# Half-height matmuls in pairs: a routed two-expert layer whose first product runs part of its terms on two halves of the TensorE array

## The chip, the cores and the metric

The kernel runs on one core of a Trainium2 chip. The metric is the device time of one execution in microseconds (us), the median of several runs.

## What is computed

The reference is a causal convolution over a sequence, followed by a mixture of experts in which each token goes to two of eight experts:

```python
# x: (8, 3584, 192), weight: (8 heads, 7 taps)
w = softmax(weight)                        # over the taps
x = causal_conv(x, w)                      # (28672 tokens, 192)
noisy = x @ w_gate + log1p(exp(x @ w_noise)) * noise    # (28672, 8)
top2, top2_w = two largest of noisy, softmax over the two
for e in range(8):
    for k in range(2):
        mask = top2[:, k] == e
        h = np.maximum(x[mask] @ w1[e], 0.0)            # 192 -> 1024
        out[mask] += top2_w[mask, k, None] * (h @ w2[e])  # 1024 -> 192
```

All inputs and outputs are float32.

## The kernel before

**The stages.** The 28672 tokens are split into 28 units of 1024. A unit is convolved (mostly on VectorE, DVE), scaled, split into float16 high and low parts in a tile `rb`, gated (eight small matmul groups on TensorE, PE, at line 485, and some 50 small DVE instructions), and its rows are scattered by indirect DMAs of GpSimd (POOL) into a DRAM buffer `xs`, which has one region for each expert. The experts' work is done in *blocks*: a round `j` has one block for each of the eight experts `e`; the blocks of round 0 have 128 tokens, those of the 28 rounds behind it 256, so 8 + 224 = 232 blocks in all. Between the blocks' instructions the convolution and the gating of later units are laid in, in two *slots* per block (`side.slot(0, ...)` and `side.slot(1, ...)`), with a budget of DVE time for each. From the fourth unit on, the gating transposes its input by eight DMAs of SyncE (SP), line 476, into a tile `xT`.

**One block.** `load_block` brings 256 rows of `xs` by one transposing DMA into a tile `bT` of three columns of 256 tokens on 128 partitions. A row of `xs` holds the high parts of x's first 128 dimensions (column 0), their low parts (column 1), and in column 2 the high parts of the other 64 dimensions on partitions 0 to 63 and their low parts on 64 to 127. The three `bT` buffers are filled two blocks ahead.

The first product, `mm1`, computes 1024 features as 8 chunks of 128, four to a *half*, each half in one PSUM tile `ph` of two banks (two such tiles in turn). Each weight is a high and a low float16 part as well; the last 64 rows of w1 stand on both halves of the partitions. A chunk is the sum of five matmuls of 128 rows by 256 tokens: high weight by high x, low weight by high x, high weight by low x (all for the first 128 dimensions), then the high weight and then the low weight of the last 64 dimensions by column 2. Behind each half, ScalarE (ACT) writes the float16 high part of the relu, `hh` (line 662), and DVE the low part, `hl` (line 663); together these are called the split here.

The second product, `mm2`, has 24 matmuls of 192 columns for each 128 tokens (48 in a block of 256), over the chunks and the three parts `(hh, high)`, `(hh, low)`, `(hl, high)`, line 673. ACT scales the result to `y` (line 676), and POOL adds it to the output by an indirect DMA (line 677).

**What sets the order.** PE, DVE, ACT and SP run in the order in which the code is written; POOL's order is the scheduler's. The second product of a block is held back by one block (`pend`), so PE's order is: first half of block n, second product of block n-1, second half of block n, and so on; the slots' own instructions stand behind each half's split:

```python
mm1(e, xT, T, 0, h[:, 0], h[:, 1])
prefetch(n + AHEAD)
...
side.slot(0, T, rate, spent)
if pend:
    mm2(*pend)
mm1(e, xT, T, 1, h[:, 0], h[:, 1])
side.slot(1, T, rate)
```

The functions that the change touches, and the loop that calls them:

Of the kernel before, what the change touches and what calls it, by code (L numbers as in the profile page):

```python
# [32 lines left out]
def kernel(  # L33
# [167 lines left out]
    def w1_part(e, c, lo, f):  # L201
        return parts(e, c)[1 + lo][:, f * P:(f + 1) * P]
# [447 lines left out]
        waited.update(range(ready[j] + 1))  # L650
        tc.add_to_no_dep_group("loads", ld.ins)

    def mm1(e, xT, T, half, hh, hl):
        nf = FC // 2
        ph = psum.tile([P, nf, BIG], F32, name="ph", bufs=2)
        for f in range(nf):
            seq = [(0, 0, 0), (1, 0, 0), (0, 0, 1), (0, 1, 2), (1, 1, 2)]
            for i, (lo, wc, c) in enumerate(seq):
                nc.tensor.matmul(ph[:, f, :T], w1_part(e, wc, lo, half * nf + f), xT[:, c, :T], start=(i == 0),  # L659
                                 stop=(i == len(seq) - 1))  # L660
        hs = slice(half * nf, (half + 1) * nf)
        halves.append(nc.scalar.activation(hh[:, hs, :T], ph[:, :, :T], AF.Relu))  # L662
        V.scalar_tensor_tensor(hl[:, hs, :T], ph[:, :, :T], 0.0, hh[:, hs, :T], op0=OP.max, op1=OP.subtract)  # L663

    def mm2(j, T, e, hh, hl, ids, gate):
        adds = []
# [21 lines left out]

    def load_block(j, e):
        start, T = rounds[j]  # L690
        xT = io.tile([P, 3, BIG], F16, name="bT", bufs=3)
        r0 = e * REG + start
        ld = nc.sync.dma_start(xT[:, :, :T], xs[r0:r0 + T, 0:384], transpose=True)
        loads(ld, j)
        return xT


# [164 lines left out]
    for n, (j, e) in enumerate(blocks):  # L862
        T = rounds[j][1]
        need = max(ready[min(i, len(rounds) - 1)] + j - i for i in range(j, j + 5))
        rate = RATES[min(max(side.gate_done - need, 0), 2)]
        if j not in metas:
            metas[j] = round_meta(j, mts.pop(j))
        ids, gate = metas[j]
        while prepared[0] < e:
            next(prep, None)  # L870
        if j == 0:
            unscale(gate[:, e:e + 1, :], slice(e, e + 1), T // P)
        xT = xTs.pop(n)
        h = ffn.tile([P, 2, FC, BIG], F16, name="h")
        mm1(e, xT, T, 0, h[:, 0], h[:, 1])
        prefetch(n + AHEAD)
        spent = 0.0
        if e == E - 1 and j + 1 < len(rounds):
            metas[j + 1] = round_meta(j + 1, mts.pop(j + 1))
            spent = 1.6  # L880
        side.slot(0, T, rate, spent)
        if pend:
            mm2(*pend)
        mm1(e, xT, T, 1, h[:, 0], h[:, 1])
        side.slot(1, T, rate)
        pend = (j, T, e, h[:, 0], h[:, 1], ids[:, e, :], gate[:, e, :])
    mm2(*pend)
# [12 lines left out]
    with tc.If(total > 0):  # L900
        ctr = small.tile([P, 1], F32, name="ctr")
        for e in range(E):
            nb = nc.values_load(noi[0:1, e:e + 1], engines=engines, min_val=0, max_val=N // P)
            V.memset(ctr, float(cap))
            with tc.For_i(0, nb, 1) as i:
                row = i * P + (e * REG + cap)
                xT = io.tile([P, 3, BIG], F16, name="bT", bufs=3)
                nc.sync.dma_start(xT[:, :, :P], xs[bass.ds(row, P), 0:384], transpose=True)
                mt = ffn.tile([P, 1, 1, 8], F32, name="mto")
                nc.sync.dma_start(mt[:, 0, 0, :], xsf[bass.ds(row, P), 192:200])  # L910
                es = slice(e, e + 1)
# [1 line left out]
                unscale(gate, es, 1)  # L913
                V.tensor_scalar(ctr, ctr, float(P), None, op0=OP.add)
                h = ffn.tile([P, 2, FC, BIG], F16, name="h")
                for half in range(2):
                    mm1(e, xT, P, half, h[:, 0], h[:, 1])
                mm2(len(rounds) - 1, P, e, h[:, 0], h[:, 1], ids[:, 0, :], gate[:, 0, :])


# [23 lines left out]
```

## Time and profile before

| | |
|---|---|
| runs | 2212.12, 2216.77, 2217.0 us |
| median | 2216.77 us |
| span of the profiled execution | 2225.0 us |
| PE busy | 2051.9 us (92%) |
| PE weight loads busy | 1907.0 us (86%) |
| DVE busy | 1527.6 us (69%) |
| POOL busy | 1339.1 us (60%) |
| ACT busy | 790.2 us (36%) |
| mean granted TensorE clock | 0.971 |

The span runs from the first to the last instruction of the one execution that was profiled; it is 0.4% longer than the median of the runs shown, and no other time of that execution is known. A matmul's own duration in the trace (273 ns for one of 256 columns) is its way through the array; matmuls follow each other more closely than that, so prices are taken from start to start. PEld is the weight load that stands ahead of each matmul and runs beside the one before it.

### The profile page before, as it was taken

The numbers are of one execution on the slowest core, as the hardware profiler recorded it, in microseconds if no ns is written. First come the engines' busy times: TensorE is split into PE (matmuls) and PEld (weight loads), VectorE is DVE, ScalarE is ACT, GpSimd is POOL, SyncE is SP. The second block draws the span as 40 slices with busy tenths as digits, with TensorE's granted clock in tenths as the row PEclk, the third lists the DMA queues.
The fourth block names the chain that finished last, engine by engine and source line by source line (L and its number), as shares of the span: only waits on it lengthen the run. The fifth ranks groups of instructions, "written<-read, shape, count | busy, mean of one in ns | idle before, by whom it ended". The sixth has DMA issues, their size and how long they took to land.

```text
span 2225.0 us, 53210 instructions
## 1 busy us (share of the span) xinstructions
PE 2051.9 (92%) x22098; PEld 1907.0 (86%) x22098; DVE 1527.6 (69%) x4018; ACT 790.2 (36%) x1154; POOL 1339.1 (60%) x923
## 2 busy tenths in 40 slices
PE   6466799899999999999999999999999999999997
PEld 5466689789888889998999999998999999999997
DVE  6488578788788767786777877777777874423332
ACT  4443233333333333333333333333333333333332
POOL 0553556676776757666666576666766676543333
PEclk8788899999999999999999999999999999999999
DMA  8523656556665655466655766456664656443342
GB/s 242 162 46 72 141 102 106 94 99 109 116 116 111 118 107 111 81 110 116 113 81 101 114 117 115 82 101 109 115 107 79 112 100 108 72 57 47 49 52 31
DMA packets 462773, 223.64 MB, mean 101 GB/s; under 512 B 342152, under 2 KB 449720, under 8 KB 462393
## 3 DMA queue, kind: packets, MB, share of 16 engines
q1 hardware_dynamic: 375352, 129.38, 28.3%
q0 software_dynamic: 87168, 90.76, 27.1%
q8 instruction: 174, 2.85, 0.5%
q14 instruction: 79, 0.65, 0.1%
HBM read 40.12 MB, written 115.38 MB: 70 GB/s over the span
## 4 chain that ended last, share of the span: by engine, by line
PE 69%; DVE 10%; SPq 3%; another core or an unknown queue 3%; ACT 3%; issue 3%; DMA 2%; POOL 1%; ACTq 0%; DVEq 0%; POOLq 0%
PE py L673 34%; PE ph L659 34%; DVE h L663 3%; SPq L476 3%; DVE xc L416 2%; ACT h L662 2%; DMA xT<-rb 1%; PE misc L485 1%; DVE xc L414 1%; ACT y L676 1%; DVE t L512 0%; DMA out_dram<-y,ids 0%; POOL xs L571 0%; DVE am L427 0%
## 5 line engine op out<-in xcount | busy, mean ns | idle before, releaser
L677 POOL DMA_INDIRECT out_dram<-y,ids x456 | 802.5, 1760 | 538.9 <-ACT y L676 357.2
L659 PE MATMUL ph<-bT,w1s 128*128 128x256 f16 (+1 forms) x9280 | 1054.7, 272 | 19.7 <-issue 14.0
L673 PE MATMUL py<-w2s,h 128*128 128x192 f16 x10944 | 972.4, 249 | 49.3 <-DVE h L663 31.1
L659 PEld LDWEIGHTS <-w1s 128*128 128x128 f16 x9280 | 891.3, 98 | 130.0 <-issue 29.9
L673 PEld LDWEIGHTS <-h 128*128 128x128 f16 x10944 | 920.4, 99 | 73.6 <-DVE h L663 40.3
L663 DVE SCALAR_TENSOR_TENSOR h<-ph,h 128x1024 f16<-128x1024 f32 (+1 forms) x464 | 557.2, 1201 | 572.8 <-ACT h L662 540.0
L571 POOL DMA_INDIRECT xs<-rb,idx x448 | 518.6, 1158 | 269.8 <-issue 198.5
L662 ACT ACTIVATE h<-ph 128x1024 f16<-128x1024 f32 (+1 forms) x464 | 467.2, 1009 | 581.3 <-PE ph L659 435.4
L416 DVE SCALAR_TENSOR_TENSOR xc<-xt,wt,xc 128x192 f32<-128x192 f32 x1260 | 430.5, 408 | 0.2 <-DMA xt<-zero 0.2
L676 ACT ACTIVATE y<-py,ga 128x192 f32<-128x192 f32 x456 | 190.9, 420 | 643.2 <-PE py L673 423.5
L414 DVE TENSOR_SCALAR xc<-xt,wt 128x192 f32<-128x192 f32 x210 | 55.8, 327 | 4.1 <-DMA xt<-in_x_dram 4.1
L485 PEld LDWEIGHTS <-xT 128*128 128x128 f16 x1120 | 34.4, 96 | 26.1 <-DMA xT<-rb 18.6
L485 PE MATMUL misc<-ghi,xT 128*128 128x16 f16 x672 | 36.0, 170 | 21.2 <-DMA xT<-rb 16.4
L427 DVE TENSOR_REDUCE am<-xc 128x8 f32<-128x1536 f32 (+2 forms) x28 | 46.9, 1674 | 0.3
L442 DVE TENSOR_TENSOR xc<-xc,xs 128x1536 f32<-128x1536 f32 (+2 forms) x28 | 47.0, 1678 | 0.0
L512 DVE SCALAR_TENSOR_TENSOR t<-t,t 128x64 f32<-128x64 f32 x168 | 39.8, 237 | 5.8
L450 DVE TENSOR_TENSOR rb<-xc,rb 128x1024 f16<-128x1024 f32 x28 | 34.6, 1237 | 12.8 <-ACT rb L447 12.4
L447 ACT ACTIVATE rb<-xc 128x1024 f16<-128x1024 f32 x28 | 29.4, 1049 | 33.2 <-DVE xc L442 13.4
L284 POOL TENSOR_TENSOR w1s<-w1s,w1s 128x1024 f16<-128x1024 f32 x5 | 10.6, 2128 | 48.2 <-DMA w2s<-in_moe_w_dram 43.0
L504 ACT ACTIVATE t<-t 128x64 f32<-128x64 f32 x28 | 7.2, 256 | 90.6 <-DVE t L502 61.8
L392 PE MATMUL ph<-xt,dg 128*128 128x192 f32 x140 | 26.4, 353 | 12.0 <-ACT dg L382 12.0
L485 PE MATMUL misc<-glo,xT 128*128 128x16 f16 x448 | 35.3, 170 | 1.2 <-issue 1.2
(143 smaller groups left out, 671.5 us busy)
## 6 DMA issues: line engine op xcount, KB each, us to landing
out_dram<-zero SPq DMA_DIRECT2D x28, 768.0 KB
xt<-in_x_dram SPq DMA_DIRECT2D x27, 768.0 KB
out_dram<-y,ids POOLq DMA_INDIRECT x456
xs<-rb,idx POOLq DMA_INDIRECT x448
w2s<-in_moe_w_dram SPq DMA_DIRECT2D x16, 384.0 KB
w1s<-in_moe_w_dram SPq DMA_DIRECT2D x8, 512.0 KB
w1s<-in_moe_w_dram SPq DMA_DIRECT2D x16, 256.0 KB
bT<-xs SPq DMA_TRANSPOSE x232
```

Source lines behind the costliest of these rows:

```text
L414: V.tensor_scalar(dst, src, wt[:, h, k:k + 1], None, op0=OP.mult)
L416: V.scalar_tensor_tensor(dst, src, wt[:, h, k:k + 1], dst, op0=OP.mult, op1=OP.add)
L442: V.tensor_tensor(v, v, xsc[:, :, None].to_broadcast([P, TU, len(hs) * G]), op=OP.mult)
L476: nc.sync.dma_start(xT[:, t], rb[:, t, 0:384], transpose=True)
L485: nc.tensor.matmul(lg[:, t], xT[:, t, c, :], g[:, gc], start=(i == 0), stop=(i == len(seq) - 1))
L571: s = nc.gpsimd.indirect_dma_start(out=xsf, out_offset=bass.IndirectOffsetOnAxis(ap=idx[:, k, t:t + 1], axis=0), in_=rbf[:, t, :], in_offs ...
L659: nc.tensor.matmul(ph[:, f, :T], w1_part(e, wc, lo, half * nf + f), xT[:, c, :T], start=(i == 0), stop=(i == len(seq) - 1))
L662: halves.append(nc.scalar.activation(hh[:, hs, :T], ph[:, :, :T], AF.Relu))
L663: V.scalar_tensor_tensor(hl[:, hs, :T], ph[:, :, :T], 0.0, hh[:, hs, :T], op0=OP.max, op1=OP.subtract)
L673: nc.tensor.matmul(py[:, :D], a[:, f, ts], w2_part(e, lo, f), start=(n == 0), stop=(n == 3 * FC - 1))
L676: nc.scalar.activation(y, py[:, :D], AF.Copy, scale=gate[:, h:h + 1])
L677: a = nc.gpsimd.indirect_dma_start(out=out, out_offset=bass.IndirectOffsetOnAxis(ap=ids[:, h:h + 1], axis=0), in_=y, in_offset=None, compu ...
```

## The change

In each chunk the fifth matmul, the low weight of the last 64 dimensions by column 2, is replaced by one of 64 rows that takes only the high parts of x; the product of low weight and low part drops out. The four 64-row matmuls of a half form two pairs: the first of a pair uses partitions (array rows) 0 to 63 and chunk 0 or 1, the second partitions 64 to 127 and chunk 2 or 3, which lies in the other PSUM bank. For the second, the high parts are needed on partitions 64 to 127, so `bT` has a fourth column, filled by a second transposing DMA. The pairs of both halves stand in a row, behind the full matmuls of the first half and ahead of those of the second, so both `ph` tiles are taken at once. The first half's split and slot 0 stand between the pairs and the second half's full matmuls, and the second product of the block before stands behind both halves.

```diff
-    def mm1(e, xT, T, half, hh, hl):
-        nf = FC // 2
-        ph = psum.tile([P, nf, BIG], F32, name="ph", bufs=2)
-        for f in range(nf):
-            seq = [(0, 0, 0), (1, 0, 0), (0, 0, 1), (0, 1, 2), (1, 1, 2)]
+    HF = FC // 2
+
+    def mm1_full(ph, e, xT, T, half, first):
+        seq = [(0, 0, 0), (1, 0, 0), (0, 0, 1), (0, 1, 2)]
+        for f in range(HF):
             for i, (lo, wc, c) in enumerate(seq):
-                nc.tensor.matmul(ph[:, f, :T], w1_part(e, wc, lo, half * nf + f), xT[:, c, :T], start=(i == 0),
-                                 stop=(i == len(seq) - 1))
+                nc.tensor.matmul(ph[:, f, :T], w1_part(e, wc, lo, half * HF + f), xT[:, c, :T],
+                                 start=(first and i == 0 and f % 2 == 0),
+                                 stop=(not first and i == len(seq) - 1), skip_group_check=True)
+
+    def mm1_pairs(ph, e, xT, T, half, first):
+        for k in range(HF // 2):
+            for q in range(2):
+                f, rows = 2 * q + k, slice(64 * q, 64 * q + 64)
+                nc.tensor.matmul(ph[:, f, :T], w1_part(e, 1, 1, half * HF + f)[rows], xT[rows, 2 + q, :T],
+                                 start=(first and k == 0), stop=not first, skip_group_check=True)
...
+    def mm1(e, xT, T, hh, hl, between):
+        ph = [psum.tile([P, HF, BIG], F32, name="ph", bufs=2) for _ in range(2)]
+        mm1_full(ph[0], e, xT, T, 0, True)
+        mm1_pairs(ph[0], e, xT, T, 0, False)
+        mm1_pairs(ph[1], e, xT, T, 1, True)
+        split(ph[0], T, 0, hh, hl)
+        between()
+        mm1_full(ph[1], e, xT, T, 1, False)
+        split(ph[1], T, 1, hh, hl)
...
-        xT = io.tile([P, 3, BIG], F16, name="bT", bufs=3)
+        xT = io.tile([P, 4, BIG], F16, name="bT", bufs=3)
         r0 = e * REG + start
-        ld = nc.sync.dma_start(xT[:, :, :T], xs[r0:r0 + T, 0:384], transpose=True)
-        loads(ld, j)
+        loads(nc.sync.dma_start(xT[:, 0:3, :T], xs[r0:r0 + T, 0:384], transpose=True), j)
+        loads(nc.sync.dma_start(xT[:, 3, :T], xs[r0:r0 + T, 192:320], transpose=True), j)
...
-        mm1(e, xT, T, 0, h[:, 0], h[:, 1])
-        prefetch(n + AHEAD)
...
+        mm1(e, xT, T, h[:, 0], h[:, 1], between)
         if pend:
             mm2(*pend)
-        mm1(e, xT, T, 1, h[:, 0], h[:, 1])
         side.slot(1, T, rate)
```

`split` holds the two lines for `hh` and `hl` that `mm1` ended with, and `between` is what stood between the first half and `mm2`: the prefetch, the metadata of the next round, and slot 0. In the changed program the full matmuls keep line 659, the 64-row ones are line 667, the relu is line 672, DVE's split 673, the second product 693, `y` 696, the output's add 697, and the block's two transposes 713 and 714.

Three places show how the order moves. First PE, where the first half of an expert's block ends (`w1s4` and `w1s5` are the weight buffers of the full and of the last 64 dimensions, `ph`, `bT`, `h` and `py` as above). Before, the last matmul of the half is followed by the second product:

```order
L659 LDWEIGHTS w1s5_137
L659 MATMUL ph_16761<-bT_16483,w1s5_137 128x256
L673 LDWEIGHTS h_16587
L673 MATMUL py_16804<-w2s2_151,h_16587 128x192
L673 LDWEIGHTS h_16587
```

And of the change, the end of the eight pair matmuls, behind which the second half's full matmuls come:

```order
L667 LDWEIGHTS w1s5_137
L667 MATMUL ph_16878<-bT_16602,w1s5_137 128x256
L659 LDWEIGHTS w1s4_136
L659 MATMUL ph_16878<-bT_16602,w1s4_136 128x256
L659 LDWEIGHTS w1s4_136
```

Between the halves no second product is left; the second half's tile is begun by the pairs.

Then ACT, in a cycle's place where a unit's float16 parts are written (`rb`). Before:

```order
L662 ACTIVATE h<-ph 128x1024 x2
L447 ACTIVATE rb_190<-xc 128x8x128
L448 ACTIVATE rb_190<-xc 128x8x64
L676 ACTIVATE y<-py,ga 128x192 x2
L662 ACTIVATE h<-ph 128x1024 x2
L676 ACTIVATE y<-py,ga 128x192 x2
```

After:

```order
L672 ACTIVATE h<-ph 128x1024
L447 ACTIVATE rb_190<-xc 128x8x128
L448 ACTIVATE rb_190<-xc 128x8x64
L672 ACTIVATE h<-ph 128x1024
L696 ACTIVATE y<-py,ga 128x192 x2
L672 ACTIVATE h<-ph 128x1024 x2
```

The two outputs `y` of the block before have moved from between the two relus of a block to behind the second.

Last SP, where a unit's transposes for the gates (`xT`) are issued, with the metadata (`mt`), the next x (`xt`) and the zeros of the output ahead of them. Before:

```order
L599 DMA mt<-xs 128x8x8 x2
L693 DMA_TRANSPOSE bT<-xs 128x3x256
L180 DMA xt<-in_x_dram 128x1536
L693 DMA_TRANSPOSE bT<-xs 128x3x256
L367 DMA out_dram<-zero 128x8x192
L476 DMA_TRANSPOSE xT<-rb_192 128x3x128 x8
```

After:

```order
L599 DMA mt<-xs 128x8x8 x2
L713 DMA_TRANSPOSE bT<-xs 128x3x256
L714 DMA_TRANSPOSE bT<-xs 128x256
L180 DMA xt<-in_x_dram 128x1536
L713 DMA_TRANSPOSE bT<-xs 128x3x256
L714 DMA_TRANSPOSE bT<-xs 128x256
L367 DMA out_dram<-zero 128x8x192
L476 DMA_TRANSPOSE xT<-rb_192 128x3x128 x8
```

One more transpose stands between the load of x and the gates' transposes, and one ahead of it.

More of the change, by code (lines that the diff above doesn't have):

```diff
@@ L651, in loads, with split @@
         tc.add_to_no_dep_group("loads", ld.ins)
-    def mm1(e, xT, T, half, hh, hl):
-        nf = FC // 2
-        ph = psum.tile([P, nf, BIG], F32, name="ph", bufs=2)
-        for f in range(nf):
-            seq = [(0, 0, 0), (1, 0, 0), (0, 0, 1), (0, 1, 2), (1, 1, 2)]
-            for i, (lo, wc, c) in enumerate(seq):
-                nc.tensor.matmul(ph[:, f, :T], w1_part(e, wc, lo, half * nf + f), xT[:, c, :T], start=(i == 0),
-                                 stop=(i == len(seq) - 1))
-        hs = slice(half * nf, (half + 1) * nf)
+    HF = FC // 2
+    def mm1_full(ph, e, xT, T, half, first):
+        seq = [(0, 0, 0), (1, 0, 0), (0, 0, 1), (0, 1, 2)]
+        for f in range(HF):
+            for i, (lo, wc, c) in enumerate(seq):
+                nc.tensor.matmul(ph[:, f, :T], w1_part(e, wc, lo, half * HF + f), xT[:, c, :T],
[7 more added lines that the diff above has]
+                                 start=(first and k == 0), stop=not first, skip_group_check=True)
+    def split(ph, T, half, hh, hl):
+        hs = slice(half * HF, (half + 1) * HF)
         halves.append(nc.scalar.activation(hh[:, hs, :T], ph[:, :, :T], AF.Relu))
         V.scalar_tensor_tensor(hl[:, hs, :T], ph[:, :, :T], 0.0, hh[:, hs, :T], op0=OP.max, op1=OP.subtract)
+    def mm1(e, xT, T, hh, hl, between):
[7 more added lines that the diff above has]
+        split(ph[1], T, 1, hh, hl)
     def mm2(j, T, e, hh, hl, ids, gate):
@@ L874, with between @@
         h = ffn.tile([P, 2, FC, BIG], F16, name="h")
-        mm1(e, xT, T, 0, h[:, 0], h[:, 1])
-        prefetch(n + AHEAD)
[L877 to L881, printed above, removed]
+        def between():
+            prefetch(n + AHEAD)
+            spent = 0.0
+            if e == E - 1 and j + 1 < len(rounds):
+                metas[j + 1] = round_meta(j + 1, mts.pop(j + 1))
+                spent = 1.6
+            side.slot(0, T, rate, spent)
+        mm1(e, xT, T, h[:, 0], h[:, 1], between)
         if pend:
             mm2(*pend)
-        mm1(e, xT, T, 1, h[:, 0], h[:, 1])
         side.slot(1, T, rate)
@@ L906 @@
                 row = i * P + (e * REG + cap)
-                xT = io.tile([P, 3, BIG], F16, name="bT", bufs=3)
-                nc.sync.dma_start(xT[:, :, :P], xs[bass.ds(row, P), 0:384], transpose=True)
+                xT = io.tile([P, 4, BIG], F16, name="bT", bufs=3)
+                nc.sync.dma_start(xT[:, 0:3, :P], xs[bass.ds(row, P), 0:384], transpose=True)
+                nc.sync.dma_start(xT[:, 3, :P], xs[bass.ds(row, P), 192:320], transpose=True)
                 mt = ffn.tile([P, 1, 1, 8], F32, name="mto")
@@ L915 @@
                 h = ffn.tile([P, 2, FC, BIG], F16, name="h")
-                for half in range(2):
-                    mm1(e, xT, P, half, h[:, 0], h[:, 1])
+                mm1(e, xT, P, h[:, 0], h[:, 1], lambda: None)
                 mm2(len(rounds) - 1, P, e, h[:, 0], h[:, 1], ids[:, 0, :], gate[:, 0, :])
```

## The prediction

> **What bounds the kernel now.** I read the page first: the busy shares, the slices, and the chain that ended last.
>
> ```profile
> PE 2051.9 (92%) x22098; PEld 1907.0 (86%) x22098; DVE 1527.6 (69%) x4018; ACT 790.2 (36%) x1154; POOL 1339.1 (60%) x923
> PE   6466799899999999999999999999999999999997
> DVE  6488578788788767786777877777777874423332
> PEclk8788899999999999999999999999999999999999
> PE 69%; DVE 10%; SPq 3%; another core or an unknown queue 3%; ACT 3%; issue 3%; DMA 2%; POOL 1%; ACTq 0%; DVEq 0%; POOLq 0%
> ```
>
> PE is busy in nine tenths or more of nearly every slice from the sixth on and holds 69% of the chain; DVE is second, with 10%. The average of DVE (69%) hides two regimes, so I then asked for stretches of one late cycle of the work, and for a stretch near the end. The columns are the stretch, its length, busy time (and count) on PE, PEld, DVE, ACT, POOL, then clock, DMA share, GB/s.
>
> ```profile
> 1242.10:1283.10 41.00, 41.00 (x473) 38.88 (x471) 39.11 (x112) 13.73 (x22) 22.01 (x16) 1.00 0.65 96
> 1283.10:1311.50 28.40, 27.56 (x290) 25.65 (x289) 14.36 (x31) 12.09 (x17) 22.20 (x18) 1.00 0.65 130
> 2002.00:2185.00 183.00, 183.00 (x1937) 173.04 (x1935) 58.30 (x77) 63.46 (x89) 68.66 (x44) 1.00 0.40 50
> ```
>
> For 41 of every 69 us DVE has work for 39.11 us: two engines are full at once there. In the 28 us behind it DVE is half idle, and near the end it has 58 of 183 us. Only in these two is PE alone the bound.
>
> The timeline of PE near the end gives the price of a block when nothing disturbs it:
>
> ```profile
> 1992.79 4.12 PE L673 MATMUL py<-w2s,h 128*128 128x192 f16 x48
> 1996.75 4.53 PE L659 MATMUL ph<-bT,w1s 128*128 128x256 f16 x40
> 2001.11 4.12 PE L673 MATMUL py<-w2s,h 128*128 128x192 f16 x48
> ```
>
> Start to start, 40 matmuls of the first product take 2001.11 - 1996.75 = 4.36 us, 0.109 us each; the 48 of the second take 3.96 us; a block is 8.32 us.
>
> **The pairs.** Of each block's 40 first-product matmuls, 32 stay and 8 become 64-row ones. What a 64-row matmul costs alone, and what it costs to go from 128 rows to 64 and back, is in the gram matrices, where 8 matmuls of 128 rows, 8 of 64 and 12 of 128 follow each other (the timeline counts the first two kinds as one group of 16):
>
> ```profile
> 97.06 1.18 PE L269 MATMUL grams<-w1s 128*128 128x128 bf16 x16
> 98.17 0.86 PE L269 MATMUL grams<-w2s 128*128 128x128 bf16 x12
> 98.88 1.18 PE L269 MATMUL grams<-w1s 128*128 128x128 bf16 x16
> 99.99 0.87 PE L269 MATMUL grams<-w2s 128*128 128x128 bf16 x12
> L269 PE MATMUL grams<-w1s 128*128 128x128 bf16 x64 | 5.4, 230 | 1.5 <-DMA w1s<-in_moe_w_dram 1.5
> L269 PE MATMUL grams<-w1s 64*128 64x128 bf16 x64 | 5.0, 217 | 0.2 <-DMA w1s<-in_moe_w_dram 0.2
> ```
>
> The last two rows: 64 rows (217 ns) are as long as 128 (230 ns), so a half-height matmul alone saves nothing. The 12 of one kind take 98.88 - 98.17 = 0.71 us, 0.059 each; the 16 take 1.11 us where 16 x 0.059 = 0.95 would do. Two changes of height cost 0.16 us by this. The 12 themselves begin with such a change, which makes 0.16 a lower bound; I take 0.19.
>
> That two matmuls on different array rows run at once no row of this trace shows. The bounds are 4 x 0.109 us for the eight (all overlap) and 8 x 0.109 (none does). Weight loads don't stand in the way, since 27 of them in a row took 0.74 us, far less than the 0.109 us that each pair has for two:
>
> ```profile
> 103.71 0.74 PEld L485 LDWEIGHTS <-xT 128*128 128x128 f16 x27 [1.69 <-ACT xT L468]
> ```
>
> I take full overlap, because the pairs write different PSUM banks and read different partitions, so I see nothing they share. A block then saves 4 x 0.109 - 0.19 = 0.245 us (8.08 instead of 8.32), and loses 0.19 without overlap. The Trainium skill, "TensorE: Matmul & The Clock Gate", section "Part 3: Packing small matmuls — row/col tiling", says that matmuls on different row groups start about 4 ns apart; by it the four pairs would take some 16 ns more than I count, an estimate, 0.23 us saved. The Trainium skill, "TensorEngine Tiling (Array Packing)", section "Key Properties", speaks against the change: going to another tiling mode drains the array. The 0.16 us above agree with it, and that the pairs of both halves share two such changes is what leaves a gain at all: with four, 0.06 us would be left.
>
> There are 224 blocks of 256 tokens: 224 x 0.245 = 55 us. The first eight, of 128, save about 4 x 0.057 - 0.19 = 0.04 us each: nothing. The DVE and ACT passes over ph keep their size.
>
> **What of the 55 us reaches the end.** DVE's instruction order is the same in both programs up to the end of the last block: first split, slot work, second split, slot work. So where DVE is full, PE only arrives earlier and waits. The rows of DVE's splits against the PE groups that release them:
>
> ```profile
> 1263.17 4.53 PE L659 MATMUL ph<-bT,w1s 128*128 128x256 f16 x40
> 1271.50 2.35 PE L659 MATMUL ph<-bT,w1s 128*128 128x256 f16 x20
> 1276.10 4.12 PE L673 MATMUL py<-w2s,h 128*128 128x192 f16 x48
> 1258.28 1.22 DVE L663 SCALAR_TENSOR_TENSOR h<-ph,h 128x1024 f16<-128x1024 f32 x1 [0.52 <-ACT h L662]
> 1275.12 1.21 DVE L663 SCALAR_TENSOR_TENSOR h<-ph,h 128x1024 f16<-128x1024 f32 x1
> 1279.02 1.22 DVE L663 SCALAR_TENSOR_TENSOR h<-ph,h 128x1024 f16<-128x1024 f32 x1
> ```
>
> A half's matmuls end, ACT's relu follows after about 0.2 us and takes 1.0, and DVE may start. The half that ends at 1276.10 is split at 1279.02, some 1.6 us later than it could be: DVE is already late. Its one wait for ACT in that run is the 0.52 us above. So of the 41 / 8.32 x 0.245 = 1.2 us that PE saves in this stretch I count 0.4, about that idle time; in the 28.4 us behind it 3.4 x 0.245 = 0.83. That is 1.2 us a cycle, and 880 to 1850 us holds 14 cycles of 69: 17 us. From 1850 to the last matmuls some 43 blocks save all: 10.5 us. From 285 to 880 us (63 blocks) DVE is as full but less regular; half, 0.12 us a block: 7.5 us. Before 285 us the blocks wait for DVE and DMA: nothing. Sum: 35 of 55 us, with 0 and 55 as its ends.
>
> **The second product moves behind both halves.** Each block's mm2 reads the block before's h. Today only one half's 2.2 us lie between that h's last matmul and mm2; now 4.1 us do, after which the split of the second half is also overtaken by an earlier mm2. What this wait costs now:
>
> ```profile
> PEld L673 <- DVE h L663: 40.3, 38, 5.0
> PE py L673 <- DVE h L663: 31.1, 33, 4.8
> 1292.52 1.02 ACT L662 ACTIVATE h<-ph 128x1024 f16<-128x1024 f32 x1 [3.27 <-remote]
> 1294.86 2.98 PE L673 MATMUL py<-w2s,h 128*128 128x192 f16 x34 [0.79 <-DVE h L663]
> ```
>
> A typical one: the relu came late, at 1292.52, and mm2 stood for about a microsecond with 14 of its 48 done. Once a cycle this happens where DVE is half idle, so it can go. Between 0 and 31 us; I take 20, as some waits will come back as waits for ph, and the last block's (its mm2 is no longer directly behind its own half) is among them.
>
> **What is later.** On SP each block issues a second transpose. The gate matmuls (L485) wait for eight transposes that stand behind these in SP's queue:
>
> ```profile
> 1301.55 1.16 ACT L374 ACTIVATE xt<-xt 128x1152 f32<-128x1152 f32 x1
> 1302.73 0.34 SPq L180 DMA_DIRECT2D xt<-in_x_dram  x1
> 1303.17 1.21 SPq L693 DMA_TRANSPOSE bT<-xs  x1
> 1305.33 13.39 SPq L476 DMA_TRANSPOSE xT<-rb  x8
> PE misc L485 <- DMA xT<-rb: 16.4, 14, 4.7
> ```
>
> The chain starts with ACT's halo copy (L374), passes x's load and a block's transpose (1.21 us) and ends in 13.39 us of transposes. One more 1.21 us stands in it now, and PE comes sooner; against that, a block's x is free sooner, since its last reader now runs ahead of mm2. For 25 units (28 less the first three, which don't use these) that is at most 25 x 1.21 = 30 us more, and at best the 16 us of waits gone. The gate matmuls lie in the stretch where DVE is late and covers most of it: I take +4 us. Of POOL's queue nothing is moved but the time at which a block's adds start (about 2 us later); it is busy 60%.
>
> On ACT the two output copies (y) now stand behind the second relu, and the halo copy behind those; ACT is busy 36%.
>
> **Sum:** -35 - 20 + 4 = -51 us. The sum is made on the profiled execution, whose span is 2225.0 us, 0.4% over the median of the runs, 2216.77; taken off that median it gives 2166 us. About 0.3% (7 us) is what can be told from no change.
>
> **Rivals.**
> - *Nothing is gained from DVE's cover, everything reaches the end*: 55 + 31 + 16 = 102 us, 2115. For it: the idle half of each cycle; against it: 39.11 of 41 us.
> - *The pairs don't overlap*: 224 x 0.19 = 43 us lost, 20 won by the order, 4 lost on SP: 2244. For it: no row shows overlap. By the Trainium skill's section on packing, named above, this would not happen; no run here shows it yet.
> - *The split of the second half becomes the bound* (the one that ends slower by its own mechanism). Its half now ends about 2 us after the first half's, but DVE still puts the slot's work ahead of it, at most
>
> ```profile
> 1243.95 5.04 DVE L416 SCALAR_TENSOR_TENSOR xc<-xt,wt,xc 128x192 f32<-128x192 f32 x15
> ```
>
> so it ends 0.2 + 1.0 + 1.2 + 5.0 + 1.2 = 8.6 us after the first half's end, and the pairs of the next block's second half need its buffer 8.1 us after it (a block). Today the same buffer and mm2 bear about 9.4 us. That is 0.5 us in each block with such a slot, up to four a cycle, 28 cycles: 112 x 0.5 = 56 us, which takes all the gain; with DVE's lag carried on to 0.8 us each it is 90 us and 2255. It decides from 0.46 us a block. For it: DVE is full there; against it: each wait lets DVE catch up, so it should be paid once a cycle (28 x 0.5 = 14 us), inside the bound that I took.
> - *The transposes cost their full 30 us*: 2217 - 55 + 30 = 2192.
>
> **Chances and range.** The forecast (2140 to 2190) 0.50; all reaches the end (under 2140) 0.15; transposes or DVE take half (2190 to 2210) 0.12; a wash 0.08; slower 0.15, of which no overlap 0.09 and the second split 0.06. So faster 0.77, same 0.08, slower 0.15. For the range I leave out the lower end of the second case and the dearer half of the last: 2112 to 2228; the likeliest case's own is 2140 to 2190.
>
> **What would show it.** Right: eight L667 matmuls in about 0.63 us between the L659 groups, changes of height included; near the end a block of 8.08 us; in the DVE-full stretch PE waits for DVE (ph, L659 or L667 behind the split); almost no second-product waits for h. Wrong: L667 matmuls 0.109 us apart; blocks over 8.4 us near the end; PE waits for L673, the split, in every heavy block; longer waits of L485 for xT.

## The result and the profile after

The changed kernel took 2202.1 us (median of 11 runs, 2195.6 to 2213.3) and the kernel before 2217.0 (11 runs): a ratio of 0.9933, 95% interval 0.9915 to 0.9952. The interval lies below 1, so the change does gain, but less than a third of the 51 us that were forecast. On the chips of the later groups the kernel before took 2184 to 2190 us, and the changed kernel, run again, stood at 0.9829 [0.9799, 0.9858] of it: 38 us. So two things are to be explained: why 38 and not 51, and why 15 in the first comparison.

The page of the first changed run, busy shares and chain:

```profile
PE 2020.6 (92%) x22098; PEld 1794.1 (81%) x22098; DVE 1524.2 (69%) x4018; ACT 790.9 (36%) x1154; POOL 1293.3 (59%) x923
PE 64%; DVE 20%; issue 4%; ACT 3%; DMA 2%; another core or an unknown queue 1%; SPq 1%; POOL 1%; ACTq 0%; DVEq 0%; POOLq 0%
```

PE is busy 31 us less, in a span that is 20.5 us shorter (2204.5 for 2225.0), and DVE's share of the chain has gone from 10% to 20%. The two stretches that the prediction looked at, in its columns:

```profile
1242.10:1283.10 41.00, 40.51 (x459) 36.27 (x456) 33.79 (x95) 14.61 (x22) 25.24 (x16) 0.96 0.54 80
2002.00:2185.00 183.00, 183.00 (x1988) 165.03 (x1986) 57.97 (x68) 65.67 (x90) 70.24 (x45) 1.00 0.42 56
```

In the second, more matmuls fit into the same 183 us (1988 for 1937). In the first, which lies elsewhere in a cycle now, PE idles and its clock was not always granted. PE's timeline near the end shows the pairs:

```profile
1997.24 4.12 PE L693 MATMUL py<-w2s,h 128*128 128x192 f16 x48
2001.20 1.91 PE L659 MATMUL ph<-bT,w1s 128*128 128x256 f16 x16
2003.04 0.61 PE L667 MATMUL ph<-bT,w1s 64*128 64x256 f16 x8
2003.59 1.92 PE L659 MATMUL ph<-bT,w1s 128*128 128x256 f16 x16
2005.35 4.12 PE L693 MATMUL py<-w2s,h 128*128 128x192 f16 x48
```

Eight pair matmuls stand 2003.59 - 2003.04 = 0.55 us before the next group; in the records the two of a pair start 4 ns apart. A block is 2005.35 - 1997.24 = 8.11 us, 0.22 less than the 8.32 before (0.224 by the median interval of the blocks near the end, 8.103 for 8.327).

What PE waits for between 285 and 2185 us, in the first changed run (in all, number of times, longest; "issue" means that nothing in the profile explains the wait, "remote" that something ended it which the profile does not name):

```profile
PE ph L667 <- DVE h L673: 44.1, 51, 3.1
PE ph L667 <- issue: 12.3, 16, 3.0
PE ph L659 <- issue: 9.1, 22, 1.1
PE py L693 <- issue: 6.4, 21, 0.9
PE misc L485 <- DMA xT<-rb: 1.4, 2, 1.3
```

and in the kernel before, the same stretch of its first run:

```profile
PE py L673 <- DVE h L663: 22.2, 26, 3.3
PE py L673 <- issue: 8.2, 19, 1.2
PE ph L659 <- issue: 7.8, 17, 1.1
PE misc L485 <- DMA xT<-rb: 5.9, 8, 1.3
PE py L673 <- ACT y L676: 5.4, 2, 4.9
```

The second product's waits for h are gone. In their place PE stands at the pairs of the second half (L667), for the split that frees their PSUM buffer. With every row of these answers, PE waits 57 us before and 75 us after: the 48 us of the pairs (0.224 us for each of some 214 blocks from 285 us on) lose 18 us to that, and 5 us more to stretches at half clock. That makes 25 us; the spans differ by 20.5.

### The profile page after: what moved, and what is told of

Read it like the earlier page. It is cut to its first block, busy times and chain, and to the rows that moved or that the text cites. A ratio compares the mean times of both kernels' runs of the same rounds, so it can differ in the third digit from the quotient of the medians.

```text
span 2204.5 us, 53502 instructions
## 1 busy us (share of the span) xinstructions
PE 2020.6 (92%) x22098; PEld 1794.1 (81%) x22098; DVE 1524.2 (69%) x4018; ACT 790.9 (36%) x1154; POOL 1293.3 (59%) x923
## 4 chain that ended last, share of the span: by engine, by line
PE 64%; DVE 20%; issue 4%; ACT 3%; DMA 2%; another core or an unknown queue 1%; SPq 1%; POOL 1%; ACTq 0%; DVEq 0%; POOLq 0%
PE py L693 29%; PE ph L659 28%; DVE xc L416 7%; DVE h L673 6%; PE ph L667 5%; ACT h L672 2%; DVE t L512 1%; PE misc L485 1%; SPq L476 1%; DMA out_dram<-y,ids 1%; DVE xc L414 1%; PE py L392 1%; DVE t L507 0%; DMA bT<-xs 0%
## 5 line engine op out<-in xcount | busy, mean ns | idle before, releaser
L697 POOL DMA_INDIRECT out_dram<-y,ids x456 | 758.8, 1664 | 594.1 <-ACT y L696 410.9
L693 PE MATMUL py<-w2s,h 128*128 128x192 f16 x10944 | 959.5, 248 | 9.9 <-issue 9.3
L659 PE MATMUL ph<-bT,w1s 128*128 128x256 f16 (+1 forms) x7424 | 904.9, 275 | 11.4 <-issue 10.3
L659 PEld LDWEIGHTS <-w1s 128*128 128x128 f16 x7424 | 704.7, 99 | 142.3 <-issue 62.9
L667 PE MATMUL ph<-bT,w1s 64*128 64x256 f16 (+1 forms) x1856 | 157.6, 272 | 74.7 <-DVE h L673 57.6
L667 PEld LDWEIGHTS <-w1s 64*128 64x128 f16 x1856 | 73.0, 94 | 142.5 <-issue 136.8
L392 PE MATMUL ph<-xt,dg 128*128 128x192 f32 x140 | 29.0, 376 | 12.3 <-ACT dg L382 12.3
```

What stands on the lines that cost most here:

```text
L659: nc.tensor.matmul(ph[:, f, :T], w1_part(e, wc, lo, half * HF + f), xT[:, c, :T], start=(first and i == 0 and f % 2 == 0), stop=(not first ...
L667: nc.tensor.matmul(ph[:, f, :T], w1_part(e, 1, 1, half * HF + f)[rows], xT[rows, 2 + q, :T], start=(first and k == 0), stop=not first, ski ...
L693: nc.tensor.matmul(py[:, :D], a[:, f, ts], w2_part(e, lo, f), start=(n == 0), stop=(n == 3 * FC - 1))
L697: a = nc.gpsimd.indirect_dma_start(out=out, out_offset=bass.IndirectOffsetOnAxis(ap=ids[:, h:h + 1], axis=0), in_=y, in_offset=None, compu ...
```

## Experiments

The ratios are to the kernel before, run in turn on the same chip; the intervals are 95%.

### The change and the kernel before on another chip

Both kernels unaltered. Why: of the kernels on the chip of the first group below, none had ScalarE passes that came late for no visible reason, and both kernels of the first comparison had dozens.

> The changed kernel itself, unaltered, on the chip of this group. In the first comparison both kernels' traces had dozens of ScalarE passes that started up to 5 us later than anything they visibly waited for (the relus and output copies, 228 us of ScalarE idle before them in the kernel before and 281 us in the changed one); the four kernels of the experiments so far had at most 12 us of these. Theory D (those late passes took the gain: the split and with it the second half's buffer comes later, which the changed order tolerates less): without them the ratio to the kernel before is 0.980 to 0.984, as with one transpose (0.9797). Theory B (the second transpose costs 1.3%): the ratio is 0.993 again, with as few late passes. Theory A alone (VectorE's slot work ahead of the second split): the ratio is 0.988 to 0.994, and only the exchanged budgets reach 0.981.

> The kernel before, unaltered, for a trace on the chip of this group. Theory D: ScalarE's late passes are few here and the time is 2180 to 2200; second-product waits for h under 15 us. Theories A and B: waits for h near the 31 us of the first trace.

Measured: 2146.7 us, 0.9829 [0.9799, 0.9858], and 2191.7 us for the profiled run of the kernel before (2185.9 is the median of 11). PE's waits from 285 to 2185 us, first of the kernel before, then of the changed one:

```profile
PE py L673 <- ACT y L676: 16.7, 2, 12.7
PE misc L485 <- DMA xT<-rb: 12.3, 16, 1.9
PE ph L659 <- DVE h L663: 5.9, 1, 5.9
PE py L673 <- DVE h L663: 5.3, 5, 1.8
```

```profile
PE ph L667 <- DVE h L673: 39.5, 53, 6.7
PE misc L485 <- DMA xT<-rb: 5.5, 8, 1.5
```

Here all waits add up to 45 us in the one and 46 in the other. These sums leave out some 0.16 us of each wait, as they begin at the modelled end of a matmul (0.273 us behind its start, where the next one starts after 0.109). Counted from start to start instead, less the undisturbed pace and with the stretches at half clock apart, PE loses 45 us in the kernel before and 54 in the changed one, and to half clock 22 and 17 us. That makes 48 - 9 + 5 = 44 us, and the spans (2189.2 and 2146.4) differ by 43. By the same count the waits of the first comparison are 81 and 102 us, so 48 - 21 - 5 = 22 us for the 20.5 of its spans. So where no passes come late, the change trades waits of several kinds for somewhat more of one kind, the pairs' wait for the second split, and what is left is most of the pairs' 48 us.

The difference between the two comparisons is in the relus. (The record does not name the chip of the first; that it is another one is inferred from the times.) I took for each half the time from the end of its matmuls, or of ScalarE's pass before, whichever is later, to the start of its relu. From 285 us on, 61 halves of the first run of the kernel before are over 0.45 us late, 96.7 us in all, and 61 halves of the first changed run, 93.5 us; in the two runs here none is. ScalarE's own waits, in the first changed run and in the one here, show it too:

```profile
ACT y L696 <- issue: 140.1, 72, 5.2
ACT y L696 <- remote: 74.6, 24, 5.0
ACT h L672 <- remote: 38.0, 12, 5.8
ACT h L672 <- issue: 28.1, 22, 2.4
```

```profile
ACT y L696 <- issue: 9.4, 6, 1.6
ACT h L672 <- issue: 3.2, 2, 1.6
```

One place in the cycle, in the first changed run:

```profile
1508.41 0.61 PE L667 MATMUL ph<-bT,w1s 64*128 64x256 f16 x8
1512.17 1.94 ACT L672 ACTIVATE h<-ph 128x1024 f16<-128x1024 f32 x2 [2.68 <-PE ph L659]
1513.23 1.22 DVE L673 SCALAR_TENSOR_TENSOR h<-ph,h 128x1024 f16<-128x1024 f32 x1 [4.14 <-ACT h L672]
1514.37 5.06 DVE L416 SCALAR_TENSOR_TENSOR xc<-xt,wt,xc 128x192 f32<-128x192 f32 x15
1519.36 1.21 DVE L673 SCALAR_TENSOR_TENSOR h<-ph,h 128x1024 f16<-128x1024 f32 x1
1520.62 0.61 PE L667 MATMUL ph<-bT,w1s 64*128 64x256 f16 x4 [3.10 <-DVE h L673]
```

and the same block in the changed run here:

```profile
1468.58 0.61 PE L667 MATMUL ph<-bT,w1s 64*128 64x256 f16 x8
1469.02 1.02 ACT L672 ACTIVATE h<-ph 128x1024 f16<-128x1024 f32 x1 [1.61 <-PE ph L667]
1471.21 5.02 DVE L416 SCALAR_TENSOR_TENSOR xc<-xt,wt,xc 128x192 f32<-128x192 f32 x15
1476.15 1.22 DVE L673 SCALAR_TENSOR_TENSOR h<-ph,h 128x1024 f16<-128x1024 f32 x1
1477.42 0.40 PE L667 MATMUL ph<-bT,w1s 64*128 64x256 f16 x4 [0.34 <-DVE h L673]
```

The row of eight pair matmuls, of which four end the first half, starts at 1508.41, and its relu only at 1512.17, 3.76 us later; here it starts 0.44 us after them. On DVE the rest follows without a gap: split, 15 taps, second split. PE waits 3.10 us instead of 0.34. Theory D, that such passes took the gain, is borne out by its ratio, though not yet shown.

### The order alone

```diff
-        seq = [(0, 0, 0), (1, 0, 0), (0, 0, 1), (0, 1, 2)]
+        seq = [(0, 0, 0), (1, 0, 0), (0, 0, 1), (0, 1, 2), (1, 1, 2)]
...
-        mm1_pairs(ph[0], e, xT, T, 0, False)
-        mm1_pairs(ph[1], e, xT, T, 1, True)
```

(and without the second transpose)

> The changed order alone: both halves of the first product and then the second product of the block before, but all five matmuls of a chunk on 128 rows, no pairs, one transpose a block. Theory A (the gain is given back where PE waits for the PSUM buffer of the second half, because VectorE puts slot work ahead of the second split, whose matmuls now end soon after the first half's): the 31 us of waits for h go, but PE waits at the second half's first matmul instead, where the changed kernel does, for 20 to 45 us; time 2205 to 2230, so no gain or a few us. Theory B (the second transpose of each block costs the missing time): the order keeps its 20 us and has no second transpose: 2190 to 2200. Theory C (dips of the clock cost it): waits at the second half under 10 us, same time as B but with more half-clock stretches.

Measured: 2173.3 us for 2190.2, 0.9940 [0.9920, 0.9961]. The times of the expectation were for a chip on which the kernel before takes 2217; by the ratio it is between theory A (0.995 and up) and B (up to 0.992). The wait has moved as A says:

```profile
PE ph L659 <- DVE h L673: 30.6, 25, 12.3
PE misc L485 <- DMA xT<-rb: 5.6, 6, 2.3
```

Theory C, with under 10 us of these waits, falls. So the order by itself brings about 13 us, where the prediction had 20: from start to start its waits are 37 us for 45 before, and half clock costs 17 us for 22. With the pairs on top the waits grow from these 37 us to the changed kernel's 54, so the pairs bring only part of their 48 us.

### The pairs alone

```diff
         mm1_pairs(ph[0], e, xT, T, 0, False)
-        mm1_pairs(ph[1], e, xT, T, 1, True)
         split(ph[0], T, 0, hh, hl)
         between()
+        mm1_pairs(ph[1], e, xT, T, 1, True)
```

(and `between` ends with the second product, as before the change)

> The pairs without the order: each half has its four full matmuls a chunk and its two pairs, with the slot work and the second product between the halves as before the change; PE goes from 128 rows to 64 and back twice a block. By the changed kernel's trace a change of height adds 0.095 us, so a block saves 4 x 0.109 - 4 x 0.095 = 0.06 us, 13 us in all: 2168 to 2182, ratio 0.992 to 0.998. Rival (the changes of height cost nothing that counts, the pairs alone give the 25 us that separate the changed kernel from the order alone): 2155 to 2165, ratio 0.985 to 0.990.

Measured: 2197.2 us for 2185.0, 1.0050 [1.0029, 1.0070]. Both expectations missed; it is slower than the kernel before. PE near the end:

```profile
1998.00 4.13 PE L693 MATMUL py<-w2s,h 128*128 128x192 f16 x48
2002.07 0.39 PE L667 MATMUL ph<-bT,w1s 64*128 64x256 f16 x4
2002.39 3.67 PE L659 MATMUL ph<-bT,w1s 128*128 128x256 f16 x32
2005.99 0.39 PE L667 MATMUL ph<-bT,w1s 64*128 64x256 f16 x4
2006.32 4.13 PE L693 MATMUL py<-w2s,h 128*128 128x192 f16 x48
```

A block is 8.32 us (8.315 by the median): four changes of height eat all but 0.012 us of the 0.436 that the overlap saves, 0.106 us each. The gates' waits for xT are 18.9 us for 12.3 before, and there are 54.6 us at half clock for 44.4 (both from 285 to 2185 us). The second transpose may be behind these; no run without it shows that. Without the pairs in one place there is no gain at all; the order is what makes the pairs worth 0.22 us a block.

### The second transpose

```diff
-                nc.tensor.matmul(ph[:, f, :T], w1_part(e, 1, 1, half * HF + f)[rows], xT[rows, 2 + q, :T],
+                nc.tensor.matmul(ph[:, f, :T], w1_part(e, 1, 1, half * HF + f)[rows], xT[rows, 2, :T],
...
-        loads(nc.sync.dma_start(xT[:, 3, :T], xs[r0:r0 + T, 192:320], transpose=True), j)
```

> The changed kernel without the second transpose of each block: both members of a pair read the third column of bT, so the second member multiplies other rows than it should (that part of the computation is changed; the instructions on PE keep their number, shapes and array rows). SP issues one transpose a block, as before the change. Theory A: the transposes hide, 2195 to 2205, within 5 us of the changed kernel. Theory B: the missing 15 to 30 us come back, 2170 to 2187.

Measured: 2143.5 us for 2190.2, 0.9797 [0.9768, 0.9826]. Beside the first comparison's 0.9933 this looks like theory B. Against the changed kernel on an undisturbed chip (0.9829 [0.9799, 0.9858]) the difference is 0.3% and the intervals overlap, so a cost of the second transpose beside the changed order is not shown; 7 us is the best value, the prediction had 4.

### VectorE's slot work: moved, and divided in other ways

The slot moved behind the second split:

```diff
-        def between():
-            prefetch(n + AHEAD)
...
-            side.slot(0, T, rate, spent)
-        mm1(e, xT, T, h[:, 0], h[:, 1], between)
+        mm1(e, xT, T, h[:, 0], h[:, 1], lambda: prefetch(n + AHEAD))
...
+        side.slot(0, T, rate, spent)
```

and the budgets, in three versions:

```diff
-    BLOCK, FREE = 8.1, (5.0, 1.4)
+    BLOCK, FREE = 8.1, (1.4, 5.0)
```

> The changed kernel with VectorE's slot-0 work (up to 5 us) and the round's bookkeeping issued behind the second split instead of between the two splits; same arithmetic, same PE order. Theory A: the waits of the 64-row matmuls for the second split (57.6 us in the changed kernel) fall under 15 us and the time to 2150 to 2175. Theory B (second transpose): nothing changes, 2195 to 2210. Theory C (clock): the waits may go, but the half-clock stretches stay and the time is over 2185.

> The changed kernel with the two slots' budgets exchanged: 1.4 us of VectorE work between the two splits and 5.0 us behind the second one, instead of 5.0 and 1.4. Theory A: the second split is at most 0.2+1.0+1.2+1.4+1.2 = 5.0 us behind the first half's end plus the 2 us of its own matmuls, so waits of the 64-row matmuls for it fall under 15 us and the time to 2150 to 2180, about that of the kernel with the slot moved. Theories B and C: 2190 to 2210.

> The changed kernel with slot budgets of 4.0 and 2.4 us instead of 5.0 and 1.4: VectorE's work ahead of the second split falls from up to 6.2 us to about 5. Theory A (in the steady part PE waits twice a cycle, 0.5 and 0.67 us, where 4.9 to 6.2 us of slot work stand ahead of the second split): these two waits go, 14 x 1.17 = 16 us, and part of those from 285 to 880 us: 2118 to 2135, ratio 0.969 to 0.977. Rival (another wait takes their place, as with the slot moved behind the second split): 2140 to 2150, ratio 0.979 to 0.984.

> The changed kernel with slot budgets of 3.2 and 3.2 us. Theory A: as with 4.0 and 2.4, or a few us better: 2115 to 2135. Rival: the gating chain, which advances a step in one slot of a block, is stretched or its matmuls wait for VectorE (44.7 us of such waits with the budgets exchanged against 15.9), and it is no better than the changed kernel: 2140 to 2150.

| kernel | us | ratio | wait of L667 for the split | of L542 for M | all waits of PE, 285 to 2185 us |
|---|---|---|---|---|---|
| changed | 2146.7 | 0.9829 [0.9799, 0.9858] | 39.5 | 0.2 | 45.9 |
| slot 0 late | 2170.7 | 0.9912 [0.9888, 0.9935] | none | 48.8 | 73.6 |
| 1.4 and 5.0 | 2146.7 | 0.9806 [0.9781, 0.9832] | 10.1 | 24.9 | 47.6 |
| 3.2 and 3.2 | 2150.9 | 0.9835 [0.9799, 0.9870] | 6.9 | 25.9 | 48.2 |
| 4.0 and 2.4 | 2153.9 | 0.9853 [0.9816, 0.9891] | 20.0 | 9.3 | 44.3 |

The row of slot 0 late and that of 1.4 and 5.0, as examples:

```profile
PE misc L542 <- DVE M L537: 48.8, 23, 3.9
```

```profile
PE misc L542 <- DVE M L537: 24.9, 18, 8.1
PE ph L667 <- DVE h L673: 10.1, 18, 2.9
```

Theory A's cause was right and its price wrong. Less work ahead of the second split does take the pairs' wait away, but the gating chain (L537 computes M, and PE's L542 counts with it) is part of that work. Put later on DVE, it is waited for by PE in its turn. With the three other budgets the sum of the waits stays within 3 us of the changed kernel's, and their times cannot be told from its time; with the slot moved whole, the waits are 28 us more and the kernel is slower. The 16 us that theory A expected of 4.0 and 2.4 did not come, though the pairs' waits fell by 19.5. No version here beats the change by what can be measured.

### Half of the convolution left out

```diff
-                else:
+                elif u < 3 or h % 2 == 0:
                     V.scalar_tensor_tensor(dst, src, wt[:, h, k:k + 1], dst, op0=OP.mult, op1=OP.add)
```

in both kernels.

> The kernel before with about half of VectorE's convolution left out: for odd heads of units 3 and later only the first tap is computed (the output of those is not the reference's); budgets, order and everything on the other engines stay. Theory A: the cycle's 41 us with VectorE full become half idle, and this kernel is 10 to 40 us faster than the kernel before. To be compared with the next kernel.

> The changed kernel with the same half of VectorE's convolution left out. Theory A (VectorE's lag takes the gain): the two light kernels differ by 45 to 65 us, that is by all of the 224 x 0.22 = 49 us of the pairs and some of the second product's waits, and the waits for the second split fall under 15 us. Theory B (second transpose): they differ by no more than the heavy ones do, 15 to 25 us.

Measured: 2149.1 and 2114.0 us, on the chip on which the two whole kernels take 2185.9 and 2146.7. The kernel before gains 37 us by it, within theory A's 10 to 40. The light kernels differ by 35 us, the whole ones by 39. Theory A wanted 45 to 65, and it is wrong there: with DVE relieved, both orders lose most of their waits (18 and 24 us are left from 285 to 2185 us), so the difference does not grow. Theory B's 15 to 25 does not hold either. That fits the reading above, in which the order mostly trades waits.

### Late relus, put in by hand

A relu that is done two or three times over, with the same input and output, delays its half by 1.02 us a pass:

```diff
+        for _ in range(late):
+            nc.scalar.activation(hh[:, hs, :T], ph[:, :, :T], AF.Relu)
         halves.append(nc.scalar.activation(hh[:, hs, :T], ph[:, :, :T], AF.Relu))
```

First on second halves (`late` is 1 or 2 in every third of blocks 17 to 191), then on first halves:

> The kernel before, in which the relu of the second half is done two or three times over (same input, same output) in every third of the blocks 17 to 191: 87 extra ScalarE passes of 1.02 us, 89 us of lateness on 58 halves, as against 94.5 us on 61 halves in the first trace of the kernel before. Theory D (late halves cost the changed order more than the old one): this kernel loses 15 to 35 us to the kernel before, 2200 to 2222. Rival (the late halves had nothing to do with the smaller gain): whatever it loses, the changed kernel with the same passes loses the same.

> The changed kernel with the same extra passes in the same blocks (58 halves, 89 us). Theory D: it loses 40 to 60 us to the changed kernel, 2187 to 2207, and stands at 0.990 to 0.995 of the kernel before with the same passes, as in the first comparison, instead of 0.983; the loss is in waits of the 64-row matmuls for the second split. Rival: it loses what the kernel before loses, and the ratio of the two stays at 0.980 to 0.985.

> The kernel before with the same 87 extra passes of 1.02 us in the same 58 blocks, but ahead of the relu of the first half (output unchanged). Theory G (what counts is how much of VectorE's order stands behind the late half: the slot work and the second split stand behind the first split, and the changed order needs the second split 1.3 us sooner): this kernel loses 10 to 40 us to the kernel before, 2196 to 2226. Rival H (late halves are not what made the first comparison smaller): no bound, but the changed kernel loses no more than this one.

> The changed kernel with the same extra passes ahead of the relu of the first half. Theory G: it loses 45 to 75 us to the changed kernel, 2192 to 2222, in waits of the 64-row matmuls for the second split, and more than the kernel before does. Rival H: it loses as little as with late second halves (5 us), or no more than the kernel before.

| 89 us of lateness on | kernel before | changed kernel |
|---|---|---|
| second halves | 1.0212 [1.0176, 1.0247], +46 us | 0.9840 [0.9802, 0.9877], +2 us |
| first halves | 1.0026 [1.0007, 1.0045], +6 us | 0.9984 [0.9964, 1.0004], +34 us |

(The losses are ratio less 1, and ratio less 0.9829, times 2186.) The wait that grows in each of the two dear cases, from its whole trace; the kernel before with late second halves, where the names are two lines further down, then the changed kernel with late first halves:

```profile
PE py L675 <- DVE h L665: 42.3, 45, 4.8
```

```profile
PE ph L667 <- DVE h L675: 81.6, 73, 4.8
```

They are 16.9 and 62.0 without the passes. Theory D said that the changed order bears any late half worse, and in that form it falls: late second halves cost it almost nothing and cost the old order half of their length. Theory G had the signs right for first halves and both sizes too high (10 to 40, and 45 to 75). What the change did is to exchange the half that matters. Before, the second half was split last and then read by the second product, 2.2 us of matmuls later. Now a second half's relu is ready while DVE is still at the slot work, and it is the first half on which everything hangs: its split, up to 5 us of slot work, and the second split that the next pairs wait for.

Then each kernel got the late halves of its own first trace back:

> The kernel before with extra passes of 1.02 us exactly where its own first trace had late relus, rounded to whole passes: 106 passes on 61 halves, 38 of them on first halves (96.7 us in the trace). Theory G: it loses 25 to 45 us, 2211 to 2231, the 31 us by which the first comparison's time (2217) lies above that on the other chips (2186). Rival H: it loses under 15 or over 55 us.

> The changed kernel with extra passes exactly where its own first trace had late relus: 93 passes on 61 halves, 78 of them on first halves (93.5 us in the trace). Theory G: it loses 40 to 60 us, 2187 to 2207, the 55 us by which its time of the first comparison (2202) lies above that on the other chip (2147), and stands at 0.988 to 0.996 of the kernel before with its own passes. Rival H: it loses under 30 us, and the ratio stays at 0.98 to 0.986.

> The changed kernel with extra relu passes of 1.02 us wherever its first trace had a relu later behind its matmuls than the same relu in the undisturbed trace, whatever held it up: 165 passes on 107 halves, 107 of the passes on first halves. Theory G (late first halves cost 34/89 = 0.38 us each us, late second halves 0.05): 107 x 0.38 + 58 x 0.05 = 44 us lost, 2185 to 2200, ratio 1.000 to 1.008 to the kernel before: then late relus account for most of the 55 us. Rival I (the rest is in PE's own late starts, 33 us in that trace, which no relu explains): under 2180, ratio under 0.997.

| kernel | passes, of them on first halves | us | ratio |
|---|---|---|---|
| before, its late relus | 106, 38 | 2212.6 | 1.0125 [1.0100, 1.0151] |
| changed, its late relus | 93, 78 | 2171.7 | 0.9933 [0.9907, 0.9960] |
| changed, all that came late | 165, 107 | 2194.9 | 1.0048 [1.0030, 1.0066] |

The kernel before loses 28 us, of the 31 by which it was slower in the first comparison. The changed one loses only 23 us with the relus that were late by themselves, where theory G wanted 40 to 60, and 48 of 55 with those too that stood behind a late output copy on ScalarE. So most of each kernel's slowness comes back. The quotient 1.0048/1.0125 = 0.9924, about 0.989 to 0.996 by both intervals, is near the 0.9933 of the first comparison, but it is not like for like. With the relus late by themselves in both kernels it is 0.9933/1.0125 = 0.981, no more than without late passes. By the rule of the last row, the first trace of the kernel before would have 139 passes on 87 halves, 54 of the passes on first halves, and no run has these. The 33 more would cost it some 10 us by the losses above (an estimate: 17 x 46/89 + 16 x 6/89), and the quotient would be about 0.988, between the two comparisons. So late passes are shown to slow both kernels by about what they lost; that they account for the whole difference of the ratios is not shown.

Two reservations more. In the first changed trace 29 of PE's 75 us of waits have nothing late to show ("issue"), and 45 are for ph; the run with all passes has none of the former, and 73 for ph. The sum agrees, its parts not wholly. And a pass on ScalarE does not hold back SP's transposes, which were late too in the first traces. Why the halves came late in the first comparison stays open. In the kernel before they stand at the same place in nearly every cycle from 880 us on, 1.8 us late on the second half of one block in eight and 0.7 on the next half. There SP's transposes, which wait for the same matmuls, start late together with the relu, as in the prediction's row at 1292.52:

```profile
1292.51 1.21 SPq L693 DMA_TRANSPOSE bT<-xs  x1
```

So the signal from PE came late, not ScalarE. The trace's records of semaphores say so too: 59 of the 61 late relus of each first run start right behind an update of the semaphore that the half's last matmul raises, typically 0.02 us, and that update comes 1.7 us (median of the kernel before) after the matmul's modelled end, where it comes 0.01 to 0.02 us after it for the other halves. PE's records show no gap there. The Trainium skill, "Perfetto Trace Analysis", section "Tensor Engine Instruction (MATMUL, LD_WEIGHTS)", says that a matmul's end is estimated and that the semaphore is pushed only when PSUM has acknowledged the bytes; that leaves room for such a delay, and no run here shows which part of it was late.

## Why the prediction was right and wrong

The step that failed is the account of PE's waits. The forecast had 20 us lost to DVE's lag and 20 won at the second product, so none on balance. In the first comparison the waits grew instead, from 57 to 75 us (81 to 102 from start to start), and on the other chip from 45 to 54 from start to start. The pairs themselves came out near their term.

- **The pairs.** Overlap, right: 4 ns apart. The eight were to take 0.63 us with both changes of height and take 0.65 (8 x 0.109 less the 0.224 that a block saves); a block 8.08 us, it is 8.10 to 8.11; 55 us, it is 48 to 50. The two changes of height cost 0.19 to 0.21 us, as taken from the gram matrices.
- **The second product's waits.** That they go was right, in every trace. The failure is beside it: of 31 us I let 20 be won, with "some waits will come back as waits for ph". Of the 31, only 22.2 lie behind 285 us. And more came back than went: in the first comparison the pairs' waits (L667) are 56 us after, 44.1 of them for the split. Without late passes, 45 us of waits before stand against 54 after, from start to start.
- **What reaches the end.** I took 20 of 55 us as lost to DVE. The pairs' wait for the second split, which the prediction knew as its third rival with 14 us ("it should be paid once a cycle"), is 11.9 us from 880 to 1850 us on the other chip, in 27 waits of up to 0.8 us, twice a cycle (16 us from start to start): near it. But 27.6 us more lie between 285 and 880 us, where the prediction had no price for it beyond half of a 15 us gain. There the terms are, from start to start, -48 for the pairs, +9 for the waits and -5 for half clock; the profiled spans differ by 43 us and the medians by 39. So the forecast's -51 was near in size for that chip, partly by luck: it counted 13 us too little for the pairs, took 20 us of waits to go where 9 came, and left out half clock, which won 5.
- **The gates' transposes.** +4 us foreseen; the waits for xT fell in both pairs of whole kernels (5.9 to 1.4 us in the first, 12.3 to 5.5 in the second; between the light ones they stayed, 13.5 and 13.8), and what the second transpose costs lies within the error.
- **The first comparison.** Here the account of the waits failed by the most. The prediction says that "ACT's relu follows after about 0.2 us", also in the 8.6 us of its third rival. In its own trace that was not so for 61 halves (over 0.45 us, 1.6 on average), and it quotes one, "3.27 <-remote" ahead of a relu at 1292.52, and reads it as a wait that the new order would hide. For a second half that is true. The same lateness on first halves, of which the old order bears 89 us for 6, costs the new one 34; and in the first changed trace 49 of its 61 late halves are first halves, for 29 of 61 before. Why they moved there is open. It was not asked on which half a late relu would fall, or what stands behind each half on DVE in the new order. The time, 2202, lies in the case "transposes or DVE take half" (2190 to 2210), but late signals from PE were no part of that case.
- **The rivals.** "Everything reaches the end" and "no overlap" are refuted by the rows above; the split of the second half did become the first wait of PE, at a little more than the price of the waits that it replaced (54 for 45 us), and so it did not turn the sign. "The transposes cost their full 30 us" does not hold: without the second one the changed kernel takes 7 us less, and the intervals overlap.

## What to carry to other kernels

When work is put in a new order, look again, half by half, at what stands behind each producer on the engine that follows: an order that removes one wait can make another tile the one on which all hangs, and lateness that cost little there becomes the bound. A late start that the trace does not explain is a row to follow up before it is counted as hidden. When operations that need a change of the array's height are added, put them side by side: here two changes of height a block left 0.22 us of the 0.44 that the overlap saves, and four left 0.01.

## What the runs showed of the hardware

- Two 64-row matmuls on different array rows, into different PSUM banks, start 4 ns apart, and the pairs follow each other at 0.109 to 0.12 us, like single matmuls of 128 rows. Each change between 128 and 64 rows adds 0.095 to 0.106 us.
- PE's clock drops to half in stretches of 3.41 us and its multiples, and short waits can be enough. In all twenty traces, of the gaps between starts of matmuls from 285 to 2170 us (less the 0.109 us of one matmul) that begin at full clock, a half-clock stretch begins in the gap or within 3.6 us behind it in 61 of 508 cases for gaps of 0.5 to 1.2 us, in 43 of 119 for 1.2 to 2 us, in 33 of 62 for 2 to 3 us, and in 61 of 62 for longer ones. The length alone does not decide it: with slot 0 late it was 5 of 21 gaps of 2 to 3 us. The Trainium skill, "TensorE: Matmul & The Clock Gate", section "Part 1: The HAM clock gate", has a free-running window of 3413 ns, and the stretches of 3.41 us agree; its section "Why this matters for your kernels" warns of gaps over about 3 us, and by these counts a stretch follows gaps of 1.2 to 3 us in 76 of 181 cases.
- The same two programs were 31 and 55 us slower in the first comparison than on the chips of the later groups, at the same pace of matmuls near the end (8.327 and 8.103 us a block in both). Both first traces have 61 late halves, 59 of them behind a late signal from PE; the later groups' eleven traces without added passes, on four chips, have none.
